# Block-sparse attention with a feed-forward layer: V's first sum of squares on TensorE, bfloat16 sums over partitions from step 48 on, and new sequences' queries started two steps sooner

## The chip, the cores and the metric

The kernel runs on one core of a Trainium2 chip. The metric is the device time of one execution in microseconds (us), here as the median of several runs.

## The reference

Attention over 4 sequences of 768 tokens with 8 heads of 64, of which each block of 32 queries sees its neighbours, the first and last block and three sampled blocks; the first and last block of queries see everything. Behind it a feed-forward layer with a leaky ReLU.

```python
def _attn_ref(q, k, v, sampled_blocks):
    scores = scale * np.matmul(q, k.transpose(0, 1, 3, 2))
    ...
    scores = np.where(mask, scores, -1000000000.0)
    scores = scores - np.max(scores, axis=-1, keepdims=True)
    attn = np.exp(scores)
    attn = attn / (np.sum(attn, axis=-1, keepdims=True) + 1e-09)
    return np.matmul(attn, v).astype(np.float32)

def _moe_ref(x, w_in, w_out):        # x: 3072 x 512, w_in: 512 x 2048
    h = x @ w_in
    g = np.maximum(0.01 * h, h)
    return (g @ w_out).astype(np.float32)
```

q, k and v are float32, the weights are doubles (64 bits).

## The kernel before

**Numbers.** Every operand of a large product is split into a float16 high part and a float16 low part, and a product is made of the parts' products. Before the split a tensor is scaled by a power of two, found from its sum of squares: squares are summed within each partition, the sums of the 128 partitions are added by a product with a matrix of ones (`scale_sum`, L133, its matmul at L135), and `scale_of` (L138) makes the scale out of the exponent on VectorE in four or five tiny steps (`tot`, `ex`, `inv`, `s`). Squares within a partition are taken in one of two ways: `square` (L227, its instruction at L230) is an ACT activation with an accumulated sum, used for Q, K and V; `squares` (L191) is used for the weights, multiplies blocks of 128 columns with themselves on TensorE in bfloat16 (the upper two bytes of each float32, read with a stride; L201), adds the diagonal with a VectorE reduction (L204), and gives one column.

**The attention** goes in units. An item is a third of a sequence (256 queries, 12 items), a tile T is 64 queries of two blocks, a unit is one tile and one pair of heads: 16 units an item, 192 steps in all. Of one unit: `scores` (L692, matmuls at L714, tile s) multiplies the queries, stacked as high and low parts (qs) and once more with the parts swapped (qxs), with the gathered keys (kg, or kt for T = 0); `unit_ttr` (L719) adds the mask and finds the maximum on VectorE (L723); `unit_exp` takes exp on ACT (L735); `unit_high` (L749) and `unit_split` (L779) divide and split (ACT L762, DVE L783, tile pp) and transpose by DMA into pt (L788); `pair_av` (L799, matmuls at L815) multiplies by the gathered values vg. In the first item the transpose is done on TensorE instead (`unit_turn`, L773).

**The feed-forward layer** goes in chunks of 256 hidden units: `ffn_h` (L850, 24 matmuls, tile h), activation (ACT L856, DVE L859 and L863, POOL L864), `ffn_o` (L877, 12 matmuls, tile o). The weights come in 1 MB or 512 KB loads (L356), are decoded from doubles (ACT L363, DVE L364 to L367), squared, scaled and split (ACT L430, DVE L435); few buffers hold raw weights, so a load waits until an earlier one is decoded.

**Q, K and V.** Queries are prepared in halves of an item (128 queries, 24 halves): `get_q` loads one (L532), `start_q` (L1033) puts `prep_q` (L582) into the list of side work: square (L587), sum, scale, split (ACT L594, DVE L596), a DMA transpose into qs (L599), and two DMA copies of qs with its halves swapped into qxs (L601, L602). Half 6 is the first of sequence 1, half 12 of sequence 2, half 18 of sequence 3. `prep_v` (L485) squares V's four pairs of heads on ACT, sums, scales, splits (ACT L505, DVE L508) and stores the result to DRAM (scr, L512), out of which rows are gathered (L676, L683).

**What sets the order.** The loop at L1139 goes through the steps and calls these parts in an order written as a string of letters. Side work advances by a given amount a step (`side_step`, L955, queries first). From step 48 (`even_at`) the chunks of the feed-forward layer are spread evenly, eight over sixteen steps, and `unit_exp` is remembered in `last_exp` (L1211), which until then is None. What the loop emits is reordered once more by a scheduler that works with priorities and its own estimates; each engine then runs its list strictly in order, and so does each DMA queue, of which SyncE's (SP) carries nearly all loads, transposes and stores. The start of queries reads:

```python
        if step % 8 == CFG["q_at"] % 8:                                    # q_at is 8
            start_q(step // 8 + (2 if CFG["q_at"] < 8 else 1))
```

Of the kernel before, what the change touches and what calls it, by code (L numbers as in the profile page):

```python
# [12 lines left out]
BF16 = mybir.dt.bfloat16  # L13
# [59 lines left out]
def tile_block_sparse_attention_ffn(  # L73
# [58 lines left out]

    def scale_sum(ss, n, name):  # L133
        pb = bank(f"{name}_sum")
        nc.tensor.matmul(pb[:, :n], ones, ss, start=True, stop=True)  # L135
        return pb

    def scale_of(pb, n, name, total=False, keep=None, fl="q"):  # L138
# [52 lines left out]
    def squares(parts, name, fl):  # L191


        now = tc.cur_priority
        tc.cur_priority = now - CFG["bs"]
        pb = bank(f"{name}_sq")
        blocks = [t.bitcast(BF16).rearrange("p (n l) -> p n l", l=2)[:, c:c + P, 1]
                  for t in parts for c in range(0, t.shape[1], P)]
        begin = len(nc.cur_bb.bb.instructions)
        for i, t in enumerate(blocks):  # L200
            nc.tensor.matmul(pb[:, :P], t, t, start=(i == 0), stop=(i == len(blocks) - 1))  # L201
        loose.update(i.name for i in nc.cur_bb.bb.instructions[begin:])
        ss = sm.tile([P, 1], F32, tag=f"ss{fl}", name=f"{name}_ss")
        nc.vector.tensor_tensor_reduce(  # L204
            out=pb[:, :P], in0=pb[:, :P], in1=eye, scale=1.0, scalar=0.0, op0=ALU.mult, op1=ALU.add, accum_out=ss)
        tc.cur_priority = now + 24
        return ss
# [19 lines left out]
    def square(out, in_, ss):  # L227

        begin = len(nc.cur_bb.bb.instructions)
        nc.scalar.activation(out, in_, AF.Square, accum_out=ss)  # L230
        behind(begin, last_exp[0])
# [253 lines left out]
    def prep_v(b):  # L485


        ss = cst.tile([P, NP], F32, name=f"ssv_{b}")
        new = lambda hp: pa.tile([P, NC, 4, D], F16, tag="v", name=f"v16_{b}_{hp}", bufs=5)
        v16 = new(0)  # L490
        for hp in range(NP):
            square(flat(v16)[:, :S], flat(vraw[b, hp]), ss[:, hp:hp + 1])
            yield 1.0
        pb = scale_sum(ss, NP, f"v{b}")
        yield 0.2
        inv, s = scale_of(pb, NP, f"v{b}", total=True, keep=f"v{b}", fl="v")
        vscale[b] = inv
        yield 0.5
        scr[b] = dr.tile([S, H * 2 * D], F16, tag="scr", name=f"scr_{b}")
        for hp in range(NP):  # L500
            raw = vraw.pop((b, hp))
            if hp:
                v16 = new(hp)
            hi, lo = v16[:, :, 0:4:3, :], v16[:, :, 1:3, :]
            nc.scalar.activation(hi, raw, AF.Copy, scale=s[:, :1])  # L505
            yield 1.0
            for h in range(2):
                nc.vector.scalar_tensor_tensor(  # L508
                    out=lo[:, :, h, :], in0=raw[:, :, h, :], scalar=s[:, :1], in1=hi[:, :, h, :],
                    op0=ALU.mult, op1=ALU.subtract)  # L510
            v16s[b, hp] = v16.rearrange("p c (h l) d -> p c h (l d)", h=2)
            nc.sync.dma_start(  # L512
                out=scr[b].rearrange("(c p) (g x) -> p g c x", p=P, g=NP)[:, hp],
                in_=v16.rearrange("p c x d -> p c (x d)"))
            yield 1.2
        scr[b, "ready"] = True
# [516 lines left out]
    def start_q(n):  # L1033
        if n < len(halves):
            start(("q", *halves[n]), prep_q(*halves[n], rq[n]))
# [103 lines left out]
    for u in units:  # L1139
# [4 lines left out]
            start_q(1)  # L1144
        if step == 6 or step % 8 == 3 and step > 8:
            get_q((step + 5) // 8 + 1)
        if step % 8 == CFG["q_at"] % 8:
            start_q(step // 8 + (2 if CFG["q_at"] < 8 else 1))
        if nb < B:
            g = it.j * 16 + ui  # L1150
            t = g - (CFG["k_at"] if b else CFG["k_at0"])
# [164 lines left out]
```

## Time and profile before

| | |
|---|---|
| time, median of 3 runs | 844.26 us (843.1 to 845.69) |
| the profiled execution | 851.52 us, span 849.8 us |
| busy in that span: PE, DVE, ACT, POOL | 749.3, 595.5, 507.6, 352.8 us |
| granted TensorE clock, mean | 0.955 of full speed |
| moved by DMA | 135.33 MB, mean 159 GB/s |

A span is the time from the first to the last instruction. PE is TensorE's matmuls, PEld its weight loads (they overlap), DVE VectorE, ACT ScalarE, POOL GpSimd, SPq the instructions by which SyncE issues DMAs. A line such as L714 is a line of the kernel before. In a timeline a row has its start, its length, engine, line, operation, output<-inputs and how many were merged, and in brackets how long the engine had stood idle and what ended that. In a row of waits stand the total, the number of times and the longest. In a row of stretches stand, for each stretch, its length and the busy time of PE, PEld, DVE, ACT and POOL (with instructions), the granted clock, the DMA engines' share and GB/s. A merged row of DMA issues also holds the queue's own waiting.

### The profile page before, as it was taken

The numbers are of one execution on the slowest core, as the hardware profiler recorded it, in microseconds if no ns is written. First come the engines' busy times: TensorE is split into PE (matmuls) and PEld (weight loads), VectorE is DVE, ScalarE is ACT, GpSimd is POOL, SyncE is SP. The second block draws the span as 40 slices with busy tenths as digits, with TensorE's granted clock in tenths as the row PEclk, the third lists the DMA queues.
The fourth block names the chain that finished last, engine by engine and source line by source line (L and its number), as shares of the span: only waits on it lengthen the run. The fifth ranks groups of instructions, "written<-read, shape, count | busy, mean of one in ns | idle before, by whom it ended". The sixth has DMA issues, their size and how long they took to land.

```text
span 849.8 us, 20081 instructions
## 1 busy us (share of the span) xinstructions
PE 749.3 (88%) x7140; PEld 500.6 (59%) x7140; DVE 595.5 (70%) x1595; ACT 507.6 (60%) x1199; POOL 352.8 (42%) x472
## 2 busy tenths in 40 slices
PE   1666675857798999999999999998999999999997
PEld 1455543545465666666666666665666666667664
DVE  5768889898777976867777777678666776651221
ACT  5757678776445766767566667675657556551211
POOL 0218356433233464646343455454244545332221
PEclk9977778989799999999999999999999999999999
DMA  9979289998756999996969999969586766662000
GB/s 198 273 218 247 73 176 240 245 260 147 168 131 106 175 213 190 203 179 146 197 154 154 196 182 186 202 130 204 119 155 150 125 149 139 125 129 35 26 1 25
DMA packets 312004, 135.33 MB, mean 159 GB/s; under 512 B 279774, under 2 KB 292063, under 8 KB 311903
## 3 DMA queue, kind: packets, MB, share of 16 engines
q1 hardware_dynamic: 305262, 113.59, 67.2%
q0 software_dynamic: 6640, 20.45, 9.3%
q8 instruction: 56, 0.92, 0.5%
q14 instruction: 46, 0.37, 0.2%
HBM read 65.58 MB, written 12.58 MB: 92 GB/s over the span
## 4 chain that ended last, share of the span: by engine, by line
PE 70%; DMA 12%; DVE 10%; issue 3%; ACT 2%; SPq 2%; POOL 0%; POOLq 0%; ACTq 0%; DVEq 0%
PE h L850 27%; PE o L877 26%; PE s L714 8%; PE av L815 7%; DMA pt<-pp 3%; DMA wbuf<-in_moe_w_out_dram 2%; DMA qxs_q<-qs_q 2%; DMA qs_q<-qa_q 2%; DVE p L723 2%; DVE pp L783 2%; PE turn L773 2%; DVE W L365 1%; DVE W L435 1%; DVE W L367 1%; PE q_sum L135 1%
## 5 line engine op out<-in xcount | busy, mean ns | idle before, releaser
L877 PE MATMUL o<-W,g 128*128 128x512 f16 x1152 | 270.9, 381 | 6.4 <-DVE ob L898 4.2
L850 PE MATMUL h<-x,W 128*128 128x256 f16 x2304 | 274.2, 277 | 0.2 <-DVE x L833 0.2
L850 PEld LDWEIGHTS <-W 128*128 128x128 f16 x2304 | 225.0, 100 | 37.7 <-issue 3.9
L864 POOL TENSOR_TENSOR g<-ht,g 128x512 f16<-128x512 f32 x96 | 116.9, 1217 | 304.5 <-DVE g L863 254.6
L735 ACT ACTIVATE p<-p,mx 128x384 f32<-128x384 f32 x208 | 126.2, 607 | 158.7 <-DVE mx L723 123.0
L877 PEld LDWEIGHTS <-g 128*128 128x128 f16 x1152 | 108.7, 98 | 125.6 <-issue 10.8
L656 POOL COPY kg<-kt 128x256 f16 x264 | 135.0, 540 | 45.0 <-issue 15.4
L783 DVE SCALAR_TENSOR_TENSOR pp<-p,r,pp 128x384 f16<-128x384 f32 x188 | 120.4, 666 | 24.9 <-ACT pp L762 23.6
L762 ACT ACTIVATE pp<-p,r 128x384 f16<-128x384 f32 x188 | 104.2, 604 | 23.9 <-DVE r L747 10.2
L723 DVE CUSTOM_DVE_ANT_0 p<-s,em,nsc 128x384 f32<-128x384 f32 x176 | 102.0, 608 | 19.8 <-PE s L714 17.1
L683 POOL DMA_INDIRECT vg<-scr,rows x88 | 91.3, 1037 | 50.4 <-issue 20.3
L859 DVE SCALAR_TENSOR_TENSOR ht<-ht 128x512 f32<-128x512 f32 x96 | 67.8, 706 | 53.3 <-ACT ht L856 52.7
L815 PE MATMUL av<-pt,vg 128*64 128x128 f16 x2112 | 82.1, 226 | 10.1 <-DMA pt<-pp 9.6
L815 PEld LDWEIGHTS <-vg 128*64 128x64 f16 x2112 | 73.4, 114 | 27.4 <-issue 21.7
L714 PE MATMUL s<-kg,qs_q 128*64 128x384 f16 x352 | 66.2, 351 | 25.0 <-DVE mx L723 22.7
L856 ACT ACTIVATE ht<-h,gd 128x512 f32<-128x512 f32 x80 | 53.8, 672 | 57.3 <-PE h L850 54.7
L714 PEld LDWEIGHTS <-qs_q 128*64 128x64 f16 x416 | 27.0, 111 | 79.2 <-issue 53.7
L714 PE MATMUL s<-kg,qxs_q 128*64 128x384 f16 x352 | 64.0, 343 | 5.4 <-DMA qxs_q<-qs_q 5.4
L747 DVE RECIPROCAL r<-sum 128x2 f32<-128x2 f32 x96 | 15.4, 161 | 60.2 <-ACT sum L746 57.8
L863 DVE CAST g<-ht 128x512 f16<-128x512 f32 x96 | 41.8, 435 | 9.4 <-PE o L877 7.2
L735 ACT ACTIVATION_READ_ACCUMULATOR p<-p,mx 128x1 f32 x208 | 39.0, 187 | 0.0
L714 PEld LDWEIGHTS <-qxs_q 128*64 128x64 f16 x416 | 26.2, 114 | 20.8 <-DMA qxs_q<-qs_q 9.7
(138 smaller groups left out, 758.0 us busy)
## 6 DMA issues: line engine op xcount, KB each, us to landing
vg<-scr SPq DMA_DIRECT2D x33, 256.0 KB
qxs_q<-qs_q SPq DMA_DIRECT2D x48, 128.0 KB
v<-in_v_dram SPq DMA_DIRECT2D x32, 192.0 KB
scr<-v SPq DMA_DIRECT2D x16, 384.0 KB
W<-in_moe_w_in_dram SPq DMA_DIRECT2D x5, 1024.0 KB
rq<-in_q_dram SPq DMA_DIRECT2D x20, 256.0 KB
out_dram<-ob SPq DMA_DIRECT2D x20, 256.0 KB
rk<-in_k_dram SPq DMA_DIRECT2D x24, 192.0 KB
```

The costliest lines, as they stand in the source:

```text
L656: nc.gpsimd.tensor_copy(out=kg[:, :, slot * BLOCK:(slot + 1) * BLOCK], in_=kt[:, :, bass.ds(off, BLOCK)])
L683: nc.gpsimd.indirect_dma_start(out=vg[:n_, c, :], out_offset=None, in_=scr[b][:, :], in_offset=bass.IndirectOffsetOnAxis(ap=rows[:n_, c - ...
L714: nc.tensor.matmul(o, a, k, start=(n == 0), stop=(n == 1)))
L723: nc.vector.tensor_tensor_reduce(out=u.p[i], in0=u.sp[i], in1=kgs[u.b, u.T][1] if u.T else zero.to_broadcast([P, KEYS]), scale=u.nsc, scal ...
L735: nc.scalar.activation(u.p[i], u.p[i], AF.Exp, scale=-1.0, bias=u.mx[:, :1], accum_out=u.pair.sum[:, u.pi, i:i + 1])
L762: nc.scalar.activation(pp[:, 0, :], p, AF.Copy, scale=u.r)
L783: nc.vector.scalar_tensor_tensor(out=pp[:, 1, :], in0=p, scalar=u.r, in1=pp[:, 0, :], op0=ALU.mult, op1=ALU.subtract)
L815: nc.tensor.matmul(o, a, m, start=(c == 0 and l == 0), stop=(c == n - 1 and l == 1)))
L850: nc.tensor.matmul(c.ph[:, i], w, x, start=(d == 0 and m == 0), stop=(d == NP - 1 and m == 2)))
L859: nc.vector.scalar_tensor_tensor(out=c.t, in0=c.t, scalar=0.01, in1=c.t, op0=ALU.mult, op1=ALU.max)
L864: nc.gpsimd.tensor_tensor(out=c.g[:, 1], in0=c.t, in1=c.g[:, 0], op=ALU.subtract)
L877: nc.tensor.matmul(o, a, w, start=(c.first and i == 0 and m == 0), stop=(c.last and i == 1 and m == 2)))
```

## The change

Three edits. `scale_sum` multiplies the upper halves of its float32 operands as bfloat16 once `last_exp` is set, which is from step 48 on. `prep_v` takes the squares of sequence 0's V with `squares`, on TensorE; the other sequences keep ACT. And the first half of a new sequence is started at step 86 (half 12) and 134 (half 18) instead of 88 and 136; half 6 and all others stay.

```diff
     def scale_sum(ss, n, name):
         pb = bank(f"{name}_sum")
-        nc.tensor.matmul(pb[:, :n], ones, ss, start=True, stop=True)
+        if last_exp[0]:
+
+            top = lambda t: t.bitcast(BF16).rearrange("p (n l) -> p n l", l=2)[:, :, 1]
+            nc.tensor.matmul(pb[:, :n], top(ones), top(ss)[:, :n], start=True, stop=True)
+        else:
+            nc.tensor.matmul(pb[:, :n], ones, ss, start=True, stop=True)
         return pb
...
-        for hp in range(NP):
-            square(flat(v16)[:, :S], flat(vraw[b, hp]), ss[:, hp:hp + 1])
+        if b == 0:
+            n = 1
+            ss = squares([flat(vraw[b, hp]) for hp in range(NP)], f"v{b}", "v")
             yield 1.0
-        pb = scale_sum(ss, NP, f"v{b}")
+        else:
+            n = NP
+            ss = cst.tile([P, NP], F32, name=f"ssv_{b}")
+            for hp in range(NP):
+                square(flat(v16)[:, :S], flat(vraw[b, hp]), ss[:, hp:hp + 1])
+                yield 1.0
+        pb = scale_sum(ss, n, f"v{b}")
         yield 0.2
-        inv, s = scale_of(pb, NP, f"v{b}", total=True, keep=f"v{b}", fl="v")
+        inv, s = scale_of(pb, n, f"v{b}", total=b > 0, keep=f"v{b}", fl="v")
...
-        if step % 8 == CFG["q_at"] % 8:
-            start_q(step // 8 + (2 if CFG["q_at"] < 8 else 1))
+
+        n = (step + 2) // 8 + 1
+        if step % 8 == 6 and n % 6 == 0 and step >= CFG["even_at"]:
+            start_q(n)
+        n = step // 8 + 1
+        if step % 8 == 0 and (n % 6 or step < CFG["even_at"]):
+            start_q(n)
```

The scheduler lays every engine's list out anew, also where the edits don't reach; lines of the changed kernel are 5 to 16 higher. Three places follow. On TensorE, toward the end of sequence 1, the sums of sequence 2's values (v2) and of its first queries (q2_0_0) stood in the list before like this, in two places a feed-forward chunk apart (av is attention's product with values, h the chunk's first product):

```order
L815 MATMUL av_1_2_0_0_6618<-pt_1_2_0_1_6378,vg0_100 64x128
L135 MATMUL v2_sum_6660<-ssv_2_6384,ones_85 128x4
L850 LDWEIGHTS W_96
L850 MATMUL h_1_0_12_6683<-x_1_0_4565,W_96 128x256
...
L815 MATMUL av_1_2_0_0_6618<-pt_1_2_0_3_6522,vg0_100 64x128
L135 MATMUL q2_0_0_sum_6813<-ss_q2_0_0_6657,ones_85 128x1
L850 LDWEIGHTS W_96
L850 MATMUL h_1_0_14_6837<-x_1_0_4565,W_96 128x256
```

and in the changed kernel like this:

```order
L826 MATMUL av_1_2_0_0_6642<-pt_1_2_0_1_6399,vg0_100 64x128
L138 LDWEIGHTS ones_85
L138 MATMUL q2_0_0_sum_6681<-ss_q2_0_0_6551,ones_85 128x1
L138 LDWEIGHTS ones_85
L138 MATMUL v2_sum_6683<-ssv_2_6406,ones_85 128x4
L861 LDWEIGHTS W_96
L861 MATMUL h_1_0_12_6706<-x_1_0_4586,W_96 128x256
```

The queries' sum has moved up to the values' sum; that sequence 3's stand alike is not shown. In bfloat16 the weight load is a row of its own; a float32 matmul makes its own loads.

On SyncE's queue at the same place, before (scr_2 is the store of V, vg a gather out of sequence 1's, pt_1_2_2_1 the transposed probabilities of a pair of units):

```order
L788 DMA_TRANSPOSE pt_1_2_1_3_6805<-pp_1_2_1_2_6653 128x12x128
L512 DMA scr_2_6815<-v16_2_0_6385 128x6x256
L512 DMA scr_2_6815<-v16_2_1_6961 128x6x256
L676 DMA vg0_100<-scr_1_3413 128x1024
L788 DMA_TRANSPOSE pt_1_2_2_1_6955<-pp_1_2_2_0_6807 128x12x128
L512 DMA scr_2_6815<-v16_2_2_7077 128x6x256
L512 DMA scr_2_6815<-v16_2_3_7208 128x6x256
L599 DMA_TRANSPOSE qs_q2_0_0_6872<-qa_q2_0_0_6658 128x8x128
L532 DMA rq_2_0_1_6877<-in_q_dram 128x8x64
L788 DMA_TRANSPOSE pt_1_2_2_3_7069<-pp_1_2_2_2_6957 128x12x128
L601 DMA qxs_q2_0_0_6874<-qs_q2_0_0_6872 64x1024
L602 DMA qxs_q2_0_0_6874<-qs_q2_0_0_6872 64x1024
```

and after the change:

```order
L799 DMA_TRANSPOSE pt_1_2_1_3_6836<-pp_1_2_1_2_6677 128x12x128
L610 DMA_TRANSPOSE qs_q2_0_0_6893<-qa_q2_0_0_6552 128x8x128
L543 DMA rq_2_0_1_6898<-in_q_dram 128x8x64
L523 DMA scr_2_6845<-v16_2_0_6405 128x6x256
L687 DMA vg0_100<-scr_1_3434 128x1024
L612 DMA qxs_q2_0_0_6895<-qs_q2_0_0_6893 64x1024
L613 DMA qxs_q2_0_0_6895<-qs_q2_0_0_6893 64x1024
L799 DMA_TRANSPOSE pt_1_2_2_1_6976<-pp_1_2_2_0_6838 128x12x128
L523 DMA scr_2_6845<-v16_2_1_6982 128x6x256
L523 DMA scr_2_6845<-v16_2_2_7098 128x6x256
L523 DMA scr_2_6845<-v16_2_3_7229 128x6x256
L799 DMA_TRANSPOSE pt_1_2_2_3_7090<-pp_1_2_2_2_6978 128x12x128
```

The queries' transpose has passed four stores, a gather and a transpose of probabilities; the swap copies have passed two transposes of probabilities and now stand ahead of pt_1_2_2_1.

On SyncE's queue in the opening (q0_1_0 is the third half of sequence 0, W and wbuf hold raw weights), before:

```order
L356 DMA W_96<-in_moe_w_out_dram 128x2x1024
L512 DMA scr_0_564<-v16_0_2_646 128x6x256
L512 DMA scr_0_564<-v16_0_3_729 128x6x256
L356 DMA W_96<-in_moe_w_in_dram 128x2x1024 x2
L599 DMA_TRANSPOSE qs_q0_1_0_968<-qa_q0_1_0_830 128x8x128
L532 DMA rq_0_1_1_973<-in_q_dram 128x8x64
L356 DMA wbuf_97<-in_moe_w_out_dram 128x2x1024
L601 DMA qxs_q0_1_0_970<-qs_q0_1_0_968 64x1024
L602 DMA qxs_q0_1_0_970<-qs_q0_1_0_968 64x1024
```

and after the change:

```order
L361 DMA W_96<-in_moe_w_out_dram 128x2x1024
L523 DMA scr_0_521<-v16_0_3_750 128x6x256
L361 DMA W_96<-in_moe_w_in_dram 128x2x1024
L610 DMA_TRANSPOSE qs_q0_1_0_989<-qa_q0_1_0_851 128x8x128
L543 DMA rq_0_1_1_994<-in_q_dram 128x8x64
L612 DMA qxs_q0_1_0_991<-qs_q0_1_0_989 64x1024
L613 DMA qxs_q0_1_0_991<-qs_q0_1_0_989 64x1024
L361 DMA W_96<-in_moe_w_in_dram 128x2x1024
L361 DMA wbuf_97<-in_moe_w_out_dram 128x2x1024
```

The second of the two loads of w_in and the load of w_out behind it have moved behind the third half's swap copies. Earlier in the same queue, the fifth load of weights has moved ahead of the second half's transpose. On DVE that third half's part of the split (L596) stood behind a decode of weights and now stands ahead of it.

More of the change, by code (lines that the diff above doesn't have):

```diff
@@ L485, in prep_v @@
     def prep_v(b):
-        ss = cst.tile([P, NP], F32, name=f"ssv_{b}")
         new = lambda hp: pa.tile([P, NC, 4, D], F16, tag="v", name=f"v16_{b}_{hp}", bufs=5)
         v16 = new(0)
-        for hp in range(NP):
-            square(flat(v16)[:, :S], flat(vraw[b, hp]), ss[:, hp:hp + 1])
+        if b == 0:
+            n = 1
+            ss = squares([flat(vraw[b, hp]) for hp in range(NP)], f"v{b}", "v")
             yield 1.0
-        pb = scale_sum(ss, NP, f"v{b}")
+        else:
[5 more added lines that the diff above has]
+        pb = scale_sum(ss, n, f"v{b}")
         yield 0.2
-        inv, s = scale_of(pb, NP, f"v{b}", total=True, keep=f"v{b}", fl="v")
+        inv, s = scale_of(pb, n, f"v{b}", total=b > 0, keep=f"v{b}", fl="v")
         vscale[b] = inv
```

## The prediction

> **What bounds the kernel now.** I read the page's totals first, then busy time by stage, because an average over the whole span hides that the kernel has two halves.
>
> ```profile
> span 849.8 us, 20081 instructions
> PE 749.3 (88%) x7140; PEld 500.6 (59%) x7140; DVE 595.5 (70%) x1595; ACT 507.6 (60%) x1199; POOL 352.8 (42%) x472
> ...
> 50.00:100.00 50.00, 32.52 (x341) 24.53 (x335) 38.46 (x92) 30.89 (x74) 22.86 (x35) 0.73 0.78 215
> 300.00:418.00 118.00, 116.90 (x1133) 77.16 (x1130) 88.08 (x240) 81.45 (x199) 64.20 (x87) 1.00 0.93 186
> 600.00:800.00 200.00, 198.79 (x1955) 132.31 (x1954) 119.87 (x306) 105.57 (x259) 80.65 (x106) 1.00 0.59 116
> ```
>
> In the window rows the columns after the length are busy time of PE, PEld, DVE, ACT and POOL, then the granted clock, the DMA share and GB/s. From 50 to 100 us TensorE works 32.5 of 50 us, so something else sets the pace there. From 300 us it works 116.9 of 118 and 198.8 of 200 at full clock, so there every TensorE microsecond is a microsecond of the kernel. The waits of TensorE after 300 us say what is left to gain:
>
> ```profile
> PE s L714 <- DMA qxs_q<-qs_q: 4.1, 2, 2.8
> PE av L815 <- DMA pt<-pp: 1.2, 1, 1.2
> ```
>
> Two waits of 4.1 us together, and one of 1.2 us: nothing else. So I split the change into what it does to the dense part (two terms that shorten TensorE's row of work, one that lengthens it) and what it does to the opening, where TensorE isn't the bound.
>
> **Term 1, sums in bfloat16.** Each sum over partitions is one product with a matrix of ones. The rows of the queries' sums, of a step with one and of a step without:
>
> ```profile
> L135 PEld LDWEIGHTS q_sum<-ss_q,ones x48: 186/189/337, 7.6 to 717.9; 128*128 128x128 f32 x48
> L135 PE MATMUL q_sum<-ss_q,ones x48: 167/271/373, 7.6 to 718.0; 128*128 128x1 f32 x48
> ...
> 396.33 0.84 PE L815 MATMUL av<-pt,vg 128*64 128x128 f16 x24
> 397.10 0.38 PE L135 MATMUL q_sum<-ss_q,ones 128*128 128x1 f32 x2
> 397.34 2.78 PE L850 MATMUL h<-x,W 128*128 128x256 f16 x24
> ...
> 410.30 0.84 PE L815 MATMUL av<-pt,vg 128*64 128x128 f16 x24
> 411.07 2.79 PE L850 MATMUL h<-x,W 128*128 128x256 f16 x24
> ```
>
> 24 query sums (24 half items) give 48 rows: a float32 product takes two passes, each with a weight load of 189 ns. Durations overlap on TensorE, so I go by starts. Without a sum, h starts 0.77 us after av; with one, the sum starts 0.77 us after av and h another 0.24 us later. A sum costs 0.24 us. By the code 27 of them run after step 48: halves 7 to 23 (17 sums), keys of sequences 2 and 3 (8), values of both (2). What one costs in bfloat16 the trace shows nowhere; the nearest row is a product on the same strided bfloat16 view, the squares of a weight:
>
> ```profile
> L201 PEld LDWEIGHTS <-W x16: 96/97/100, 48.3 to 49.2; 128*128 128x128 bf16 x16
> L201 PE MATMUL wi_sq<-W x16: 218/218/221, 48.4 to 49.3; 128*128 128x128 bf16 x16
> ...
> 48.43 1.08 PE L201 MATMUL wi_sq<-W 128*128 128x128 bf16 x16
> ```
>
> Sixteen in 1.08 us, of which the last one's own 0.22 is tail: (1.08 - 0.22)/15 = 0.057 us each, with 128 columns where a sum has 1. Bounds for a bfloat16 sum: 0.05 us (as in that row, little more than its weight load's share) and 0.12 us (one of two float32 passes; if no pass were cheaper than now, half would go). I take 0.07, near the row of the same form: 27 x 0.17 = 4.6 us saved, bounds 27 x 0.12 = 3.2 and 27 x 0.19 = 5.1. Nothing hides this time, since the sums stand in TensorE's own line of work; after the sum only tiny DVE steps wait.
>
> The Trainium skill ("FP8 and Floating Point Precision", Matmul Precision) gives true FP32 four passes through the array; the trace has two rows a sum. By four passes a bfloat16 sum would cost a quarter of 0.24 us, and the term would be 4.9 us.
>
> **Term 2, queries two steps sooner.** Queries of a new sequence are started at steps 86 and 134 instead of 88 and 136. Both waits above are at these places: the first scores of sequences 2 and 3 stand ready but for the swapped copy qxs.
>
> ```profile
> 416.38 0.51 PE L714 MATMUL s<-kt,qs_q 128*64 128x384 f16 x3
> 418.24 0.49 PE L714 MATMUL s<-kt,qxs_q 128*64 128x384 f16 x3 [1.34 <-DMA qxs_q<-qs_q]
> ...
> 589.10 0.51 PE L714 MATMUL s<-kt,qs_q 128*64 128x384 f16 x3
> 592.38 0.82 PE L714 MATMUL s<-kt,qxs_q 128*64 128x384 f16 x3 [2.77 <-DMA qxs_q<-qs_q]
> ...
> 418.24:422.24 4.00, 4.00 (x53) 3.40 (x53) 1.99 (x7) 1.91 (x6) 1.16 (x1) 1.00 1.37 227
> 592.38:597.91 5.53, 5.53 (x53) 4.47 (x53) 1.41 (x5) 1.92 (x6) 0.53 (x1) 0.70 1.02 203
> ```
>
> The last two rows hold the same 53 matmuls behind each wait: 4.00 us at clock 1.00, 5.53 us at 0.70. So the second wait costs 1.53 us more through the clock. Term 2 is 1.34 + 2.77 + 1.53 = 5.6 us, if qxs is early enough. How early, the chain of sequence 2 says (the value sum's place on TensorE, then SyncE's queue):
>
> ```profile
> 389.89 0.39 PE L135 MATMUL v_sum<-ssv,ones 128*128 128x4 f32 x2
> ...
> 409.03 1.23 SPq L599 DMA_TRANSPOSE qs_q<-qa_q  x1
> ...
> 411.13 2.30 SPq L788 DMA_TRANSPOSE pt<-pp  x1
> 413.53 0.53 SPq L601 DMA_DIRECT2D qxs_q<-qs_q  x1
> ```
>
> In the new order the query sum stands right ahead of the value sum, at 389.9 instead of 397.1: 7.2 us sooner. On SyncE the transpose passes all four stores of V and the two swap copies pass two pt transposes. Late by 1.3 and 2.8, sooner by 7 or more: the waits go whole. What is late next is pt of unit 2_2_1, whose transpose now stands behind qxs; its slack is in the rivals. The other instructions of the moved step (a square and a scaling on ACT, some small steps and the second half of the split on DVE, the load of the next queries on SyncE) only change places within two steps, on engines busy 88 (DVE) and 81 (ACT) of 118 us.
>
> **Term 3, more changes of kind.** A scheduler laid TensorE's line out anew, and it now splits more groups. Counted in both orders from the first sum after step 48, neighbouring matmuls are of different kinds 392 times before and 403 after. One change costs:
>
> ```profile
> 402.99 0.33 PE L714 MATMUL s<-kg,qs_q 128*64 128x384 f16 x2
> 403.16 0.33 PE L714 MATMUL s<-kg,qxs_q 128*64 128x384 f16 x2
> 403.42 0.83 PE L850 MATMUL h<-x,W 128*128 128x256 f16 x6
> ```
>
> 0.26 us from the last pair of s to h against 0.17 us from pair to pair: 0.09 us. 11 x 0.09 = 1.0 us lost.
>
> **Term 4, the opening.** V's first squares leave ACT (four of 0.83 us) for TensorE (24 products at 0.057 to 0.12 us, 1.4 to 2.9 us, in a stretch with room) and one small DVE step. TensorE stood 3.8 us for them:
>
> ```profile
> L230 ACT ACTIVATE v<-v x4: 825/834/843, 32.4 to 40.9; 128x768 f16<-128x768 f32 x4
> ...
> 41.87 0.38 PE L135 MATMUL v_sum<-ssv,ones 128*128 128x4 f32 x2 [3.82 <-ACT v L230]
> ```
>
> But that wait lies where TensorE has nothing else to gain by. What the new order moves here is SyncE's queue, and weights come through it. Rows for the place where it matters:
>
> ```profile
> 69.37 0.37 SPq L356 DMA_DIRECT2D W<-in_moe_w_in_dram  x1
> ...
> 72.81 1.24 SPq L599 DMA_TRANSPOSE qs_q<-qa_q  x1
> ...
> 74.73 2.32 SPq L356 DMA_DIRECT2D wbuf<-in_moe_w_out_dram  x1
> 80.70 0.47 SPq L601 DMA_DIRECT2D qxs_q<-qs_q  x1
> ...
> 74.73 13.71 DMA wbuf<-in_moe_w_out_dram
> ...
> 83.10 1.10 ACT L363 ACTIVATE W<-W 128x1024 f32<-128x1024 f32 x1
> ...
> 65.75 1.23 DVE L365 SCALAR_TENSOR_TENSOR W<-W 128x1024 int32<-128x1024 int32 x1
> ...
> 68.09 1.22 DVE L367 SCALAR_TENSOR_TENSOR W<-W 128x1024 int32<-128x1024 int32 x1
> ```
>
> The weight load issued at 69.37 and the one at 74.73 now stand behind the swap copies of the third half, which waited 7.9 us for their transpose (72.81 to 80.70). That half's own DVE step now runs ahead of a decode (1.23 + 1.22 = 2.5 us), so the transpose goes at about 70.3, the copies at 78.2, both loads at 79.3. Two loads of 1 MB (256 rows of 512 doubles each) at the stage's 215 GB/s take 9.8 us: the second lands at 89.1 where it landed at 74.73 + 13.71 = 88.4, the first between 84 and 89 where its decode started at 83.1. So +0.7 us on the one, +1 to +6 on the other. Against that, ACT has up to 4 x 0.83 = 3.3 us more. I take +1.5 us; bounds -3.3 and the whole wait, 79.3 moved to 80.70 + 1.1 = 81.8, less 69.37: +12.4.
>
> **Sum.** -4.6 - 5.6 + 1.0 + 1.5 = -7.7 us. The profiled execution took 851.52 us (span 849.8), 7.3 us above the median of the runs, 844.26; the dense part, where the saving lies, runs at full clock in both, so I carry the difference over whole: 844.3 - 7.7 = 836.6 us. A measurement of this kernel can tell about 0.3% from no change, 2.5 us: faster is below 841.7, slower above 846.8.
>
> **Rivals.**
>
> *The weight loads slip (slower).* If the third half's transpose waits as long as before, both loads go 12.4 us late, at 81.8. The weights are a chain (load, decode, load into what that frees), and the dense part can't start before its last link. Terms 1 to 3 then give 9.2 back: 844.3 + 12.4 - 9.2 = 847.5. It decides once the slip passes 9.2 us. For it: the 13.71 us wait is on the chain that ended last. Against: that half's DVE step has moved ahead of a decode. Chance 0.10.
>
> *The opening gains.* V is scaled sooner, ACT is freed, the fifth load of weights passes the second half's transpose, and the slip doesn't appear: -3.3 instead of +1.5 gives 831.8. For it: the 3.82 us wait for ACT. Against: DVE, at 38.5 of 50 us there, is not relieved. Chance 0.16.
>
> *A bfloat16 sum costs what a float32 sum does* (its time is the change of tile shape around it, not its passes): term 1 is 0, 841.2. For it: 0.24 us is far above one column's work. Against: two passes with 189 ns loads fill it, and the wi_sq row runs at 0.057. Chance 0.09.
>
> *The wait at the new sequence only changes its name.* qxs stands ahead of pt on SyncE and holds it until qs has landed (409.03 to 413.53, 4.5 us). If the scaled queries come late, av waits for pt where s waited for qxs: term 2 gone, 842.2. For it: av's 1.2 us wait for pt shows that pt has little slack at a new sequence. Against: at the trace's times the swap copies would be issued well ahead of the pt transpose of that place. Chance 0.09.
>
> *The clock dips anyway.* If the 0.70 at 592 is not the wait's doing (something in the records before it), 1.5 us of term 2 stay: 838.1. For it: the wait is only 2.77 us long, and the 1.34 us wait left the clock at 1.00. Against: 0.70 stands right behind the longer wait, and 1.00 is the mean of the stages before and after. Chance 0.06. The Trainium skill ("TensorE: Matmul & The Clock Gate", What's actually happening) has the clock fall to half only after an idle window of about 3.4 us; by that rule this rival is right, while the row speaks for a shorter window.
>
> **How the numbers follow.** The forecast, 836.6, has 0.50; its own range with the bounds of terms 1 and 4 (opening from -1 to +5) is 833 to 841. The others have 0.10, 0.16, 0.09, 0.09 and 0.06. The range reaches down to the opening's gain with term 1 at its best and the 1.2 us wait for pt gone too, 831.8 - 0.5 - 1.2 = 830.1, and up to the loss of term 2 with term 1 at its worst, 842.2 + 1.4 = 843.6. Faster by over 0.3%: the forecast and the clock rival but for 0.01 (0.55), the opening's gain (0.16), some of the two one-term rivals, which stand at 841.2 and 842.2 (0.07): 0.78. Slower: 0.08 of the weight loads' slip, and 0.02 for a smaller slip beside a lost term: 0.10. The rest, 0.12, is the same.
>
> **What would show it right or wrong.** In the profile after: float32 sums only until step 48, and 27 single rows behind it with 0.05 to 0.12 us between a sum's start and h's; 0.24 would be the third rival. Scores at the starts of sequences 2 and 3 without a wait for qxs and a clock of 1.00 behind them; a new wait of av for pt there would be the fourth. From the first sum after step 48 to the end 9 us less. The value sum of sequence 2, at 389.9 us before, has nine of the shorter sums ahead of it (9 x 0.17 = 1.5 us) and the opening's 1.5 us: it should stand within 387 to 393. At 400 the weight loads have slipped, at 385 the opening has gained. The prediction is wrong if the dense part does not shrink by at least 6 us, or if the opening moves by more than 5 us.

## The result, and the profile after

The change makes the kernel slower: 856.85 us median of 6 runs (853.33 to 861.51) against 847.38 us of before (843.1 to 853.96), ratio 1.0133 with a 95% interval of 1.0089 to 1.0176. On other chips the same two kernels gave 854.59 against 844.31 us, ratio 1.0103 (1.006 to 1.0147). The prediction said 836.6 us, faster. Executions of one kernel scatter by about 1% here; the medians are of all of them, while the ratios, which decide, leave out the most disturbed ones of both kernels (the profile of whole_q_order, below, is of such a one), so a ratio can point another way than two medians.

The page's totals after:

```profile
span 853.2 us, 20062 instructions
PE 753.7 (88%) x7137; PEld 500.5 (59%) x7137; DVE 593.2 (70%) x1596; ACT 506.4 (59%) x1191; POOL 349.8 (41%) x472
```

Busy time by stage, the same windows as before (length, busy time of PE, PEld, DVE, ACT, POOL, then clock, DMA share, GB/s):

```profile
50.00:100.00 50.00, 33.66 (x336) 26.91 (x333) 40.54 (x92) 31.26 (x76) 24.02 (x35) 0.72 0.74 215
300.00:418.00 118.00, 117.90 (x1149) 77.07 (x1147) 89.91 (x244) 82.27 (x201) 66.11 (x89) 1.00 0.97 191
600.00:800.00 200.00, 197.70 (x1941) 131.18 (x1937) 122.17 (x308) 105.73 (x261) 78.43 (x105) 0.99 0.61 119
```

TensorE is as busy as it was, so the mean says nothing. The waits of TensorE after 300 us do:

```profile
PE av L826 <- DMA pt<-pp: 5.1, 2, 2.8
PE s L725 <- DVE mx L734: 2.0, 1, 2.0
PE h L861 <- ACT ht L867: 1.0, 1, 1.0
PE s L725 <- DMA qxs_q<-qs_q: 0.9, 1, 0.9
```

That is 9.0 us where before had 5.3 (mx is a unit's maximum from VectorE, ht a chunk's activation). The waits for qxs at the starts of sequences 2 and 3 are gone, and av waits for pt instead; the other three waits lie in one stretch, 505 to 530 us. Behind both new waits the clock falls:

```profile
445.88 1.86 PE L826 MATMUL av<-pt,v 128*64 128x128 f16 x48 [2.81 <-DMA pt<-pp]
...
624.16 1.09 PE L826 MATMUL av<-pt,v 128*64 128x128 f16 x20 [2.30 <-DMA pt<-pp]
...
440.00:450.00 10.00, 7.19 (x83) 4.63 (x81) 6.83 (x19) 5.24 (x15) 3.38 (x7) 0.85 1.13 193
620.00:630.00 10.00, 7.70 (x80) 4.69 (x79) 6.62 (x18) 6.05 (x17) 3.51 (x7) 0.83 1.11 220
```

10 x 0.15 + 10 x 0.17 = 3.2 us are lost to the clock there. Before had one such place.

The sums did get cheaper. A query's sum of the new kind, between its neighbours on TensorE, and the rows of all 27:

```profile
L138 PE MATMUL q_sum<-ss_q,ones x17: 167/178/179, 256.9 to 721.4; 128*128 128x1 bf16 x17
L138 PE MATMUL k_sum<-ss_k,ones x8: 163/178/179, 289.6 to 516.6; 128*128 128x1 bf16 x8
L138 PE MATMUL v_sum<-ssv,ones x2: 164/164/165, 389.7 to 568.5; 128*128 128x4 bf16 x2
...
425.65 0.18 PE L138 MATMUL q_sum<-ss_q,ones 128*128 128x1 bf16 x1
425.69 0.27 PE L861 MATMUL h<-x,W 128*128 128x256 f16 x1
```

0.04 us from the sum's start to that of h, where it was 0.24. The value sum of sequence 2 stands at 389.7, as before.

To divide a run I take the seventeenth VectorE row that takes the maximum of h; it belongs to the same group of h in every kernel here. Its rows before and after:

```profile
296.13 0.68 DVE L859 SCALAR_TENSOR_TENSOR ht<-ht 128x512 f32<-128x512 f32 x1
```

```profile
297.34 0.68 DVE L870 SCALAR_TENSOR_TENSOR ht<-ht 128x512 f32<-128x512 f32 x1
```

From its start to the end of the span (the dense part) it was 849.8 - 296.13 = 553.7 us before and 853.2 - 297.34 = 555.9 after: 2.2 us more, where the prediction's terms 1 to 3 had 9.2 less. Working it out: 24 of the sums lie behind that row, 24 x 0.20 = 4.8 saved; waits 3.7 more; the clock 3.2 instead of 1.7 lost, 1.5 more; changes of kind by the prediction 1.0 more: +1.4 together, so 0.8 us remain unexplained.

The two profiled executions are only 3.4 us apart while the medians are 9.5 apart. The rest is in the part before that row, the opening, and one profile doesn't show it: nine profiled executions with V's squares on ScalarE and the opening laid out on SyncE as before reach the row between 285.6 and 296.1 us, 290.3 in the mean, and the profile of before is the slowest of them. The three with the change's opening (after, and the runs whole and squares below) reach it between 292.1 and 297.3 us, 295.0 in the mean. What an edit does to the opening is read from sets of runs, below.

### The profile page after: what moved, and what is told of

It reads as the page before. It is cut to its first block, busy times and chain, and to the rows that moved or that the text cites. A ratio compares the mean times of both kernels' runs of the same rounds, so it can differ in the third digit from the quotient of the medians.

```text
span 853.2 us, 20062 instructions
## 1 busy us (share of the span) xinstructions
PE 753.7 (88%) x7137; PEld 500.5 (59%) x7137; DVE 593.2 (70%) x1596; ACT 506.4 (59%) x1191; POOL 349.8 (41%) x472
## 4 chain that ended last, share of the span: by engine, by line
PE 47%; DVE 8%; DMA 6%; ACT 4%; issue 2%; SPq 1%; DVEq 0%; ACTq 0%
PE o L888 20%; PE h L861 18%; PE av L826 5%; PE s L725 5%; DMA pt<-pp 3%; DMA qs_q<-qa_q 2%; DVE pp L794 2%; DVE p L734 2%; ACT p L746 1%; DVE v L519 1%; DVE ht L870 1%; DMA qxs_q<-qs_q 1%; ACT ob L906 0%; ACT pp L773 0%; ACT v L235 0%
## 5 line engine op out<-in xcount | busy, mean ns | idle before, releaser
L888 PE MATMUL o<-W,g 128*128 128x512 f16 x1152 | 277.1, 386 | 6.9 <-DVE ob L909 4.9
L861 PEld LDWEIGHTS <-W 128*128 128x128 f16 x2304 | 222.4, 99 | 39.9 <-issue 4.9
L794 DVE SCALAR_TENSOR_TENSOR pp<-p,r,pp 128x384 f16<-128x384 f32 x188 | 122.7, 679 | 24.8 <-ACT pp L773 22.6
```

Of the source, the lines that this page charges most:

```text
L794: nc.vector.scalar_tensor_tensor(out=pp[:, 1, :], in0=p, scalar=u.r, in1=pp[:, 0, :], op0=ALU.mult, op1=ALU.subtract)
L861: nc.tensor.matmul(c.ph[:, i], w, x, start=(d == 0 and m == 0), stop=(d == NP - 1 and m == 2)))
L888: nc.tensor.matmul(o, a, w, start=(c.first and i == 0 and m == 0), stop=(c.last and i == 1 and m == 2)))
```

## The experiments

Each run stands against the kernel before on the same chip. "Opening" and "dense" are the two parts of its profiled execution, divided at the row named above.

| run | ratio | 95% interval | median, before's | opening | dense |
|---|---|---|---|---|---|
| before | | | | 296.1 | 553.7 |
| after | 1.0133 | 1.0089 to 1.0176 | 856.85, 847.38 | 297.3 | 555.9 |
| sums | 0.9957 | 0.9908 to 1.0006 | 848.98, 844.31 | 292.8 | 550.3 |
| squares | 1.0072 | 1.0027 to 1.0117 | 853.31, 844.31 | 292.1 | 555.8 |
| queries | 0.9966 | 0.9927 to 1.0005 | 842.1, 844.31 | 287.5 | 552.5 |
| whole | 1.0103 | 1.006 to 1.0147 | 854.59, 844.31 | 295.5 | 556.2 |
| squares_old_queue | 1.0191 | 1.0134 to 1.0247 | 860.03, 845.05 | 301.1 | 555.8 |
| before_new_queue | 1.0067 | 1.0033 to 1.0101 | 849.27, 845.05 | 288.0 | 555.7 |
| sums_queries | 1.0029 | 0.9993 to 1.0065 | 844.47, 845.05 | 288.6 | 552.1 |
| sums_old_queue | 1.0054 | 1.0012 to 1.0096 | 849.2, 845.05 | 288.9 | 556.7 |
| sums_old_order | 1.0043 | 1.0007 to 1.0078 | 844.75, 842.22 | 295.2 | 552.4 |
| squares_old_order | 1.0044 | 1.0008 to 1.008 | 846.37, 842.22 | 290.0 | 551.7 |
| sums_queries_q_order | 0.9975 | 0.9934 to 1.0016 | 838.45, 842.22 | 285.6 | 552.8 |
| whole_q_order | 1.001 | 0.9968 to 1.0053 | 845.4, 842.22 | 294.1 | 554.2 |
| weights_late | 1.0115 | 1.0073 to 1.0157 | 849.6, 844.33 | 293.0 | 558.4 |
| squares_late | 1.0024 | 0.9987 to 1.0061 | 844.09, 844.33 | 282.3 | 552.6 |
| sums_queries_av | 0.9949 | 0.9905 to 0.9992 | 836.1, 844.33 | 288.0 | 545.8 |
| all_three_mended | 0.9977 | 0.9936 to 1.0019 | 840.21, 844.33 | 290.2 | 550.0 |
| whole_loads_early | 1.0273 | 1.023 to 1.0316 | 867.15, 845.75 | 307.7 | 558.8 |
| sums_queries_av_again | 0.9888 | 0.984 to 0.9935 | 835.73, 845.75 | 290.3 | 546.1 |

### One part alone

Each of the first three keeps one hunk of the diff: `scale_sum`, `prep_v`, or the starts of the queries in the main loop. The fourth is the whole change again.

**sums.** 

> Only the bfloat16 sums from step 48 on; squares of V and starts of the queries as before. Theory 1 (order): the 27 sums themselves save 27 x 0.20 = 5.4 us, but the scheduler, which takes shorter sums into account, lays the queues out anew. SyncE now issues the swap copies of half 16 ahead of the pt transpose that stood ahead of them, and a square of keys then holds ScalarE for about 5 us near 510 us. So the saving is lost there: the time is within 3 us of before (ratio 0.996 to 1.004), and the trace shows TensorE idle for 3 to 4 us in all between 500 and 535 us, none of it before. Theory 2 (opening): the loss of the whole change comes from the order of the opening, which this kernel has as before: 5 us faster, ratio 0.993 to 0.995, and no such stretch. Theory 3 (early queries): likewise 5 us faster.

**squares.** 

> Only the squares of V of the first sequence on TensorE; sums in float32 and queries as before. This kernel has the whole change's order in the opening: the weight loads behind the swap copies of half 3. Theory 1 (order): the opening takes what it took, within 2 us of before (ratio 0.998 to 1.002). Theory 2 (opening): this edit alone makes most of the loss, 8 us or more slower, ratio 1.008 or above, and the evacuations of the first items stand later in its trace. Theory 3 (early queries): within 2 us.

**queries.** 

> Only the queries of sequences 2 and 3 two steps sooner; sums in float32 and V as before. Theory 1 (order): the waits of the scores for qxs at 418 and 592 us go; waits of av for pt of 2.8 and 2.3 us with a dip of the clock come in their place near 446 and 624 us only if this edit makes them, and then the ratio is 1.00 within 0.003; if they are not there, 4 to 6 us faster, ratio 0.993 to 0.996. Theory 2 (opening): 4 to 6 us faster. Theory 3 (early queries): this edit alone makes most of the loss, by work that stands in the way at a new sequence: ratio 1.006 or above.

**whole.** 

> The whole change once more, beside its three parts on the same chip. All theories: slower by 0.9 to 1.8 per cent, ratio 1.009 to 1.018, as before. If the parts add up, the sum of their three differences gives this one; theory 1 says that they need not, since each edit lays the order out anew.

The squares of V, which I held for harmless, are the only part that loses by itself: 1.0072, a little less than theory 2 said (1.008 or above). The queries' gain, 2.2 us by the medians, isn't clear of noise, and their waits for qxs turn into 3.4 us of waits for pt. For the sums ratio and medians disagree, so their sign is open; their trace has 2.0 us of waiting for mx near 522 us, 2.4 for qxs and 2.4 for pt. Whether the parts add up depends on what is compared. By the medians their differences come to 11.5 us and the whole has 10.3. By the ratios the three come to 0.9957 x 1.0072 x 0.9966 = 0.9995 and the whole to 1.0103, so that the loss would come with their meeting, which is what theory 1 (the new order) says; with intervals of half a per cent on each part this isn't shown. Theory 3 fell, and theory 2 had the right edit.

### Is it the edit or the order?

The scheduler lays every engine's list out anew for any edit. Order edges that don't synchronise, added behind the program, tie an engine's instructions into a given list:

```python
    for first, then in zip(row, row[1:]):
        tc.add_manual_dep(by_name[then], first, mybir.DependencyInfo(
            mybir.DependencyClass.NoSync, mybir.DependencyReason.DATA), reason="order")
```

First SyncE's list alone, the other engines left to the scheduler, beside one more combination of edits.

**squares_old_queue.** 

> V's squares on TensorE as in the run squares, but SyncE's instructions are tied into the order that they have before the change (the row of order edges is added behind the program; nothing else is edited, and the other engines are laid out anew around it). Theory A (SyncE's order): the loss of the squares, 6 to 9 us, comes from SyncE's order in the opening, so it goes: ratio 0.996 to 1.003. Theory B (the other engines' order, or the squares themselves): it stays, ratio 1.005 to 1.012.

**before_new_queue.** 

> The kernel before, with ScalarE's squares, but SyncE's instructions tied into the order that the run squares has. Theory A (SyncE's order): the loss comes with the order alone: ratio 1.005 to 1.012. Theory B (the other engines' order, or the squares themselves): no loss, ratio 0.997 to 1.003.

**sums_queries.** 

> The change without V's squares: bfloat16 sums and the earlier queries, the opening as before. If the parts add up: 0.9957 x 0.9966 = 0.992, 6.5 us faster. If the order that both together make (qxs of half 16 ahead of the pt transpose, near 505 us) costs 4 to 6 us, as the trace of the whole change has it: ratio 0.996 to 1.001.

**sums_old_queue.** 

> The bfloat16 sums alone, with SyncE's instructions tied into the order that they have before the change. The 27 shorter sums are worth 5.4 us. If SyncE's order near 510 us is what took part of that in the run sums, the whole of it shows here: ratio 0.991 to 0.995, and TensorE has no waits between 500 and 535 us. If TensorE's own order, which is laid out anew in both, takes it: the ratio of the run sums, 0.9957, or above, and the waits stay.

before_new_queue came as theory A has it, 1.0067: another order on one queue, with not one operation changed, costs by the ratios what the squares cost. In its one profile the loss isn't in the opening (288.0 us) but in 8.1 us of TensorE's waits after 300 us. squares_old_queue, at 1.0191, is worse than either theory: the old order of one queue is no mend. That a queue's order fits only the lists of the other engines that it was laid out with would explain it, but no run tested that. sums_queries, at 1.0029, lies above both of its forecasts. sums_old_queue, at 1.0054, kept waits near 504 and 523 us (1.3 and 1.1 us), so SyncE's order at half 16 alone isn't what makes the waits there; I had that wrong.

### All five engines in a given order

Now the row of edges holds all five engines' lists, so that only the content differs. Operations that the other kernel doesn't have are left free.

**sums_old_order.** 

> The bfloat16 sums alone, with the instructions of all five engines tied into the order that they have before the change (order edges behind the program, nothing else edited): the content of the edit without the new layout. Theory A (order): the sums themselves are worth 27 x 0.20 = 5.4 us, and what ate it was the layout: 4 to 6 us faster, ratio 0.993 to 0.996, and the trace has before's waits, at qxs of 2.8 us near 590 us among them, and no others. Theory B (content: something in the bfloat16 products themselves costs elsewhere): ratio 0.998 to 1.006, as the runs sums and sums_old_queue have it.

**squares_old_order.** 

> V's first squares on TensorE, with all instructions that both kernels have tied into the order before the change on all five engines; the 24 new products stand in one row where the value sum stood. Theory A (order): the 6 to 9 us that the run squares lost come from the layout of the opening and are gone: ratio 0.996 to 1.002. Theory B (content: the products themselves, with what they hold up on TensorE and VectorE): ratio 1.005 to 1.010.

**sums_queries_q_order.** 

> Bfloat16 sums and earlier queries, with all five engines tied into the order of the run queries (0.9966). Theory A (order): the sums' 5.4 us come on top of the 2.9 us of the queries: ratio 0.989 to 0.992, about 837 us by a median of before of 845; this would be the fastest of the series. Theory B (content): 0.996 to 1.003, as the run sums_queries.

**whole_q_order.** 

> The whole change, all three edits, with the instructions of all five engines tied into the order of the run queries, the 24 products of V in one row where the value sum stood. Theory A (order): 0.988 to 0.993, what the prediction said of the whole change (0.991), since only the layout of the opening and of half 16 was in its way. Theory B (content): V's squares cost 6 us or more in any order: 0.998 or above.

Theory A fell for the sums: in before's own order, with 4.8 us less work on TensorE, the dense part is only 1.3 us shorter, and the runs aren't faster (1.0043). Where the time went stands first in the waits of TensorE after 300 us, 6.2 us where before had 5.3:

```profile
PE s L719 <- DMA qxs_q<-qs_q: 4.6, 2, 2.6
PE av L820 <- DMA pt<-pp: 0.9, 2, 0.6
PE s L719 <- DVE mx L728: 0.7, 1, 0.7
```

then in the clock, which now falls at the start of sequence 2 as well, behind a wait of 1.96 us. The first row is of sums_old_order, the second of before:

```profile
412.00:422.00 10.00, 8.04 (x66) 5.17 (x65) 5.67 (x16) 5.61 (x17) 4.53 (x6) 0.83 1.09 232
...
412.00:422.00 10.00, 8.66 (x85) 6.13 (x83) 7.49 (x20) 5.97 (x17) 5.66 (x9) 1.00 1.20 246
```

Longer waits (0.9 us) and the clock (10 x 0.17 = 1.7 us) take 2.6 of the 3.5 us that are missing. Even the 1.3 us may be scatter: squares_old_order and squares_late (below), which have before's order and float32 sums behind that row, took 551.7 and 552.6 us there, with the clock never down. The chain that ended last (start, length) tells the same: in before's trace it runs all but through TensorE alone from 418 to 586 us, and here it leaves TensorE several times, first for SyncE's queue:

```profile
433.68 1.01 DVE qa_q L601
...
434.72 3.09 DMA qs_q<-qa_q
...
437.82 0.48 SPq L606
...
438.35 0.59 SPq L607
...
439.03 5.72 DMA pt<-pp
```

TensorE comes sooner to places whose data doesn't. In the order of the run queries the same happens at pt: the waits for it, 3.4 us in queries, are 6.1 here, and the clock behind them is lower at both places:

```profile
434.88 1.38 PE L820 MATMUL av<-pt,v 128*64 128x128 f16 x22 [2.99 <-DMA pt<-pp]
...
609.73 2.56 PE L820 MATMUL av<-pt,v 128*64 128x128 f16 x44 [3.14 <-DMA pt<-pp]
...
430.00:440.00 10.00, 7.01 (x77) 4.71 (x75) 6.05 (x17) 5.33 (x15) 2.95 (x7) 0.83 1.01 165
605.00:615.00 10.00, 6.86 (x76) 4.47 (x73) 5.77 (x17) 5.53 (x15) 3.15 (x7) 0.83 1.03 172
```

So sums_queries_q_order, at 0.9975, came into theory B's range, and so did whole_q_order, at 1.001. But the whole change stands at 1.0103 in its own layout and at 1.001 in this one, with intervals that don't overlap, so most of its loss hangs on the layout. And squares_old_order, at 1.0044 between its theories, still loses 4.2 us by the medians in before's order, so V's products cost something themselves or by their place, which the edges left free.

### The last two causes apart

Why the products of V cost shows on TensorE. In the opening before, the query sum of half 2:

```profile
32.38 0.43 PE L135 MATMUL q_sum<-ss_q,ones 128*128 128x1 f32 x2
```

and after, with the last of the four groups of V's products ahead of them:

```profile
37.87 0.52 PE L206 MATMUL v_sq<-v 128*128 128x128 bf16 x6
39.79 0.38 PE L140 MATMUL v_sum<-v_ss,ones 128*128 128x1 f32 x2 [1.41 <-DVE v_ss L209]
40.03 0.36 PE L140 MATMUL q_sum<-ss_q,ones 128*128 128x1 f32 x2
```

The value sum gains 2 us (41.87 before, as the prediction shows it), and half 2's sum loses 7.6. `squares` takes one of three banks where the program is written, `bank` gives them out in that order, and `prep_v` now asks at its first step instead of its fifth, ahead of half 2. So half 2's sum stands behind products that wait for V's loads.

For the av, two groups were exchanged in TensorE's list at sequences 2 and 3: the first 48 products of av behind the 12 of o that followed. In squares_late, V's row asks later:

```diff
         if b == 0:
             n = 1
+            for _ in range(NP):
+                yield 1.0
             ss = squares([flat(vraw[b, hp]) for hp in range(NP)], f"v{b}", "v")
-            yield 1.0
```

**weights_late.** 

> The kernel before, every engine in its own order, with one thing moved: on SyncE the load of weights that is issued near 69 us and the one near 74 us stand behind the swap copies of half 3, where the change has them. Theory S (the rival of the prediction: the weight loads slip): this alone costs the opening 4 us or more, ratio 1.004 to 1.010, and the sums of the weights after it stay late until the dense part. Theory R (ring: the loss of the opening comes from V's products, which stand ahead of the sum of half 2 in the three banks that sums, squares and h share): within 2 us of before, ratio 0.998 to 1.003.

**squares_late.** 

> V's first squares on TensorE, but written four small steps later in V's row of work, so that half 2's sum takes its bank ahead of them as before the change, and with every engine in the order before the change (products and their reduction stand where the value sum and its reduction stood). Theory R (ring): the loss of 3.6 to 8.7 us that the squares had in three layouts is gone: ratio 0.994 to 1.002, and the sum of half 2 stands at 31 to 33 us as before, where the run squares has it at 40. Theory C (the products themselves cost, wherever they stand): ratio 1.004 or above.

**sums_queries_av.** 

> Bfloat16 sums and earlier queries in the order of the run queries, as in the run sums_queries_q_order (0.9975), with two groups changed on TensorE: the first av of sequence 2 and of sequence 3 (48 products each) stand behind the 12 products of o that followed them. There TensorE waited 3.0 and 3.1 us for pt, each followed by some 7 us at a clock of about 0.83. Theory A (the time that the sums save is spent waiting at these two places): both waits shrink to about 0.4 us and the clock stays at 1.00 behind them, 5 us for the waits and 3 us for the clock: ratio 0.986 to 0.991. Theory B (another wait takes their place right behind, at o, h or the second av): ratio 0.995 to 0.999, with waits of 2 us or more within 20 us of these places.

**all_three_mended.** 

> All three edits of the change with both mends: V's products written later as in the run squares_late, every engine in the order of the run queries, and the first av of sequences 2 and 3 behind the o that followed. Theories A and R together: as sums_queries_av or up to 2 us faster, ratio 0.984 to 0.991. If V's products cost by themselves (theory C): 4 us or more above sums_queries_av.

**whole_loads_early.** 

> The whole change with every engine in the change's own order, but on SyncE the two loads of weights near 74 us stand where they did before the change, ahead of half 3's transpose and ahead of its swap copies. Theory S (the loads that slip cost 5 to 10 us, as in weights_late): the loss shrinks from 1.010 to 1.013 by 0.005 or more: ratio 1.000 to 1.006, and the second sum of the second weights stands near 94 to 97 us rather than at 101 to 103. Theory T (these loads wait for buffers that later decodes free, so their place on SyncE sets nothing in this order): ratio 1.008 to 1.014.

**sums_queries_av_again.** 

> The fastest kernel of the series once more, on another chip's turn: bfloat16 sums and earlier queries, the order of the run queries, the first av of sequences 2 and 3 behind the o that followed. If its gain is the mechanism and not the luck of one set: ratio 0.990 to 0.997 again, and again no waits of 2 us or more after 300 us.

squares_late has half 2's sum back at its place, ahead of all 24 products:

```profile
32.71 0.42 PE L135 MATMUL q_sum<-ss_q,ones 128*128 128x1 f32 x2
...
37.90 1.55 PE L201 MATMUL v_sq<-v 128*128 128x128 bf16 x24
```

and no measurable loss: 1.0024, medians 844.09 and 844.33. So in this order the products cost nothing that the runs can tell, and bring no gain either. weights_late says that the prediction's rival can be real too: two loads of weights behind half 3's swap copies, with nothing else moved, came out at 1.0115, a little above theory S; by the medians that is 5.3 us. But its one profile has 4.7 us of that in the dense part, as 2.3 us more of waits and one more fall of the clock (1.7 us, behind a wait of 2.63 us for pt near 622 us), and none in the opening, so how they act stays open. whole_loads_early fell out of both its theories. In the change's own order the buffers of these loads come free late, and in front of the transpose they hold SyncE:

```profile
61.17 15.00 SPq L361 DMA_DIRECT2D W<-in_moe_w_in_dram  x2
76.27 1.32 SPq L610 DMA_TRANSPOSE qs_q<-qa_q  x1
```

That the scheduler put them behind was the lesser evil. No run separates what the late query sum and the late loads cost in the change, but the traces speak for the query sum. In after the two loads went out at 74.59 and 75.00 us, only 5.2 and 0.3 us later than before. And before_new_queue has the same order on SyncE with the squares on ScalarE. The second of the sums of w_in's squares on TensorE, in after and in before_new_queue:

```profile
102.59 0.38 PE L140 MATMUL wi_sum<-wi_ss,ones 128*128 128x1 f32 x2
...
93.04 0.47 PE L135 MATMUL wi_sum<-wi_ss,ones 128*128 128x1 f32 x2 [0.65 <-DVE wi_ss L204]
```

In squares and whole it stands at 101.1 and 102.0 us, in squares_late at 91.8, in sums and queries at 93.3 and 91.7. But weights_late has it at 98.9, and before itself, whose opening is the longest of the nine, at 98.3.

sums_queries_av is the version that beats both kernels: 0.9949 and, a second time, 0.9888, medians 836.1 and 835.73 us. The two places and the waits after 300 us:

```profile
426.00:436.00 10.00, 10.00 (x110) 6.37 (x107) 7.28 (x16) 5.90 (x16) 4.51 (x6) 1.00 1.01 183
600.00:610.00 10.00, 10.00 (x104) 6.02 (x100) 8.47 (x17) 6.11 (x15) 5.38 (x8) 1.00 0.93 209
...
PE o L882 <- DVE g L868: 1.1, 3, 0.5
PE s L719 <- DVE mx L728: 1.0, 2, 0.7
PE o L882 <- POOL g L869: 0.2, 1, 0.2
```

No wait for pt, the clock at 1.00, and the dense part at 545.8 and 546.1 us instead of 552.8: 7.0 us for the exchange of two groups, where the waits (7.2 in all to 2.3) and the clock (3.4 us) account for 8.3. By the medians the gain over before grows from 3.8 us (sums_queries_q_order) to 8.2 and 10.0. So it is at these two places that the saving was lost, as theory A says, though its range (0.986 to 0.991) was missed the first time and met only the second, which came out better than it was forecast (0.990 to 0.997). all_three_mended missed what both theories together had: at 0.9977 it is 4.1 us by the medians above sums_queries_av, the mark that was set for V's products costing by themselves. Its trace has the difference in the dense part, where those products don't stand: 6.3 us of waits instead of 2.3, of them 2.7 for pt. Why they are back stays open.

## Why the prediction was wrong, step by step

- **"There every TensorE microsecond is a microsecond of the kernel."** This is the step that failed, and terms 1 and 2 rest on it. The window rows show that TensorE is busy all the time, not how soon its data is there. In the prediction's own rows it waits for data at three places of the new sequences (1.34, 2.77 and 1.2 us): what is saved ahead of such a place becomes a longer wait there, and a longer wait can bring the clock down. 4.8 us saved come back as 1.3 at most (sums_old_order), and the change made the dense part 2.2 us longer where 9.2 less were forecast.
- **Term 1, the sums.** The size was right: 0.20 us each, forecast 0.17. "Nothing hides this time" was not: it is hidden by waits until the two av groups are moved.
- **Term 2, the queries.** The waits for qxs went whole, as forecast, and the clock behind them came back. The rival "the wait only changes its name", with a chance of 0.09, is what happened: 5.1 us for pt after. I had looked for it at the pt behind the first half's swap copies; it came behind those of the second half. At sequence 2 these copies went out at 438.21 us and the pt transposes behind them at 439.43, as before (438.00 and 439.36), while TensorE was ready for that av 1.4 us sooner (443.1 us, where before began it at 444.5), and the transposes took longer to land (6.4 us, where before's, for which av didn't wait, took 5.2 at most). At sequence 3 TensorE was no sooner; there the copies went out at 618.75 instead of 613.66 us, and the pt transposes at 619.96 instead of 615.79.
- **Term 3.** Carried in the sum above at 1.0 us; no run tested it by itself.
- **A term that wasn't there:** 3.9 us of waits between 505 and 530 us. The edit doesn't reach that place; the new layout does. ScalarE stands 4.93 us, where it stood 1.64 in before's trace, before a square of keys whose buffer the transpose of the previous keys holds:

```profile
510.17 2.84 SPq L585 DMA_TRANSPOSE kt<-k_k  x1
...
515.60 0.84 ACT L235 ACTIVATE k_k<-rk 128x768 f16<-128x768 f32 x1 [4.93 <-DMA kt<-k_k]
```

- **Term 4, the opening.** Mis-sized: forecast +1.5, measured only as a rest: 10.3 us by the medians for the whole, or 8.7 by the ratio, less 2.5 in the dense part, so 6 to 8 us; the means of the profiled openings differ by 4.7. The bounds (to +12.4) held it. I costed the products, ScalarE and the weight loads (at 79.3 us, where they went out at 74.6 and 75.0), and not what the products take a bank from. The place of the value sum of sequence 2, 389.7 us, passed my test for the opening by luck: before's profile has the longest opening of the nine, so a place at 389.9 us was already late.
- **Carrying the profile's difference to the median** was a further error, and so was the 0.3% taken for noise: the opening of one profiled execution spreads over 10 us at one and the same order.

## What to carry to other kernels

A bound read from busy shares needs the slack of the next chain beside it: before you book time saved on the busiest engine, look at the places where it waits today and at those where its data lands just ahead of it, and expect the saving to stop there. Under a scheduler an edit's price is content plus a new layout, and here the layout was the larger part (1.0103 against 1.001 in another layout); tie the old order down to measure the content, then mend the two or three places where the trace still waits. A product that takes a bank from a ring stands ahead of whoever asks later, however short it is.

## What the runs showed of the hardware

- **The clock falls to half behind many waits of 2 to 4 us.** In windows of 2 us, behind the wait of 2.99 us in sums_queries_q_order:

```profile
434.00:436.00 2.00, 1.12 (x22) 1.12 (x24) 0.43 (x1) 1.08 (x3) 1.20 (x3) 0.73 1.15 273
436.00:438.00 2.00, 2.00 (x34) 1.55 (x31) 2.00 (x7) 1.28 (x5) 0.00 (x0) 0.50 0.49 120
438.00:440.00 2.00, 2.00 (x10) 0.91 (x9) 1.37 (x4) 1.77 (x7) 0.61 (x1) 0.92 1.03 158
```

That is 0.50 for some 3.4 us, and 2 x (0.27 + 0.50 + 0.08) = 1.7 us lost, the same each time but for 3.4 us behind the wait of 3.88 us in sums_old_queue. In all runs but one (sums_queries, where two waits of 0.83 and 1.01 us follow each other) every such stretch after 300 us, up to the last matmul, stands behind a wait of TensorE of 1.94 us or more. Not every such wait brings one: of 30 waits of 1.94 to 3.95 us in the 20 traces, 21 did. In whole a wait of 3.05 us near 444 us left the clock at 1.00, and one of 2.00 near 527 halved it. The Trainium skill ("TensorE: Matmul & The Clock Gate", What's actually happening) tells of half rate and of a free-running window of about 3.4 us; the depth and the length agree with these rows, while an idle time of a whole window isn't needed here.
- **A transpose held SyncE longer where transfers were slow.** The same pt transpose in the same order took 10.37 us to issue in the run whole and 3.87 in squares, while the DMA engines were full in both but moved 95 and 343 GB/s:

```profile
128.00:132.00 4.00, 0.90 (x16) 0.82 (x16) 4.00 (x11) 3.51 (x9) 1.03 (x1) 0.99 1.22 95
...
129.85 10.37 SPq L799 DMA_TRANSPOSE pt<-pp  x1
```

```profile
128.00:132.00 4.00, 4.00 (x61) 2.54 (x62) 4.00 (x12) 1.85 (x6) 3.36 (x5) 1.00 1.05 343
...
130.47 3.87 SPq L794 DMA_TRANSPOSE pt<-pp  x1
```

In after, again in the same order, it took 9.71 us. How much of the opening's scatter this makes wasn't separated, and what slows the transfers in one execution and not in another, no run here tells.
